# An xLSTM-like attention with a dense layer and eight experts on one core: another pairing of token blocks, another order of the first expert series, and 32-row parts on another engine

## The chip, the cores and the metric

The kernel runs on one core of one Trainium2 chip. A core has five engines that run beside each other, each with an instruction queue that it works through in order: TensorE (PE; its weight loads are shown apart as PEld), VectorE (DVE), ScalarE (ACT), GpSimd (POOL) and SyncE (SP), which here only issues transfers. The metric is device time in microseconds (us) of one execution, as the median of several runs.

## What is computed

Three parts follow one another, all in float32. Cut to what matters:

```python
# attention: 2 batches x 8 heads, 768 steps, head size 40, a scan over t
m_new = max(f_gate + m, i_gate); f, i = exp(f_gate + m - m_new), exp(i_gate - m_new)
C = f * C + i * outer(v, k);  n = f * n + i * k
y = sigmoid(o_gate) * (C @ q) / max(abs(n . q), 1)
# dense layer: x is 1536 tokens x 320
h = x @ w_in;  x = max(0.01 * h, h) @ w_out              # 320 -> 2048 -> 320
# experts: 8 of them, 320 -> 1024 -> 320
P = exp(x @ w_gate - max)                                # 1536 x 8
for _ in range(8):
    P /= P.sum(1) + 1e-9;  P /= P.sum(0) + 1e-9;  P *= 1536 / 8
out = sum(P[:, e] * (relu(x @ w1[e]) @ w2[e]) for e in range(8))
```

## The kernel before

Products of float32 matrices are made from a rounded part and what rounding left over: a value is split by ScalarE into a "high" copy and by VectorE or GpSimd into a "low" difference, and several matmuls add up high and low terms in one PSUM bank.

**Stage 1** (to about 280 us) holds attention and the dense layer. Attention is cut into 12 chunks of 128 tokens, 6 to a batch. The dense layer goes over six tiles j of 256 tokens; each tile takes 16 steps f over the 2048 inner columns, so there are 96 steps g = 16 j + f. A step has eight matmuls up (`ha`, line 201), a leaky relu on ScalarE (`leak`, `gg`, line 668), the split (`hha` on ScalarE, line 674, `hla`, line 679, on GpSimd from g = 32 on), and three steps later six products down for each of the tile's two blocks (`ya`, lines 208 to 210). From g = 32 on, work that doesn't belong to the dense layer hangs at a step, before or after its down: attention of the chunks 6 to 11 by the table `ATTEND` (a chunk's steps for decay, scores, values, rest and turn, counted from the first step of the tile before the one that it fills), and the preparation of the experts by calls of `step(g, function, ...)`. A chunk's values step has the products `yps` with the weighed scores (line 563; VectorE weighs them at line 553, writing to the large buffer `R`), `zps` (569) and `dps` (575), the state.

```python
            before[g_values] += [c.values, c.recall, c.state]
            after[g_values].append(c.attend_all)
```

**Stage 2** holds the experts. Each of the 8 experts is 4 units of 256 inner columns (`NU` = 32 units); the 1536 tokens are two halves q of three positions p, a position being a pair of 128-token blocks, so there are 64 series (n, q), in a fixed list that begins (0,0), (1,0), (2,0), (0,1), (1,1), (2,1). An in-series, `up_c(i)`, makes the hidden values of a unit by seven products of four matmuls (`b`, lines 963 to 966) in place of eight, with sums and differences of the blocks of both operands. Between the products ScalarE copies `s0` (line 988), VectorE adds `s1` (991), `s2` (994) and `c11`, `c10`, `c01` (982), ScalarE makes two relu copies of each (983, 984) and GpSimd the low part (985). An out-series, `down_c(i)`, makes six blocks `y` of 320 columns by six matmuls each, and VectorE adds them to `acc` (lines 1030 to 1036; the very first ones are plain copies, on ScalarE at line 1032 for the second half). In-series i + 1 runs ahead of out-series i.

Both operands need preparing. A position (class `Position`) copies part of its tokens (`repeat`, lines 733 and 1049), turns them by eight transposes (`px`, line 286, copied at 287), makes sums (line 293), and splits: high (258), low (261), and a 32-row part of its own, `rest7`, line 265, since half of the 320 columns is 128 + 32. A unit (class `Products`) does the same with its first weight, `load1`, `sums` (line 237) and `split1`, and with the second `load2` (line 230) and `split2`, high on ScalarE (249) and low (250). In stage 2 such work is hung at slots of a series by `when(g, slot, ...)`: slots 0 to 6 follow the products of in-series g + 1, slots 7 to 12 the blocks of out-series g. There the order of the code is the order of each queue. The weights P are made in stage 2 too: logits, row sums and column sums over 8 rounds hang at slots, and P is used from the second expert on.

Of the kernel before, what the change touches and what calls it, by code (L numbers as in the profile page):

```python
# [8 lines left out]
F32 = mybir.dt.float32  # L9
# [5 lines left out]
ALU = mybir.AluOpType  # L15
# [7 lines left out]

ATTEND = ((0, 2, 6, 11, 14), (5, 6, 10, 11, 14), (0, 3, 6, 8, 14), (5, 7, 8, 12, 14))
RUNS = ((0, 0, 6), (1, 0, 10), (0, 6, 14), (1, 10, 16), (0, 14, 16))
# [29 lines left out]
def mlstm_moe_kernel(ctx, tc, qp, q3, kp, kn, vn, gates_in, og, cst_in, scr_in, w_in, w_out, w_gate, w1, w2, out):  # L55
# [156 lines left out]
    class Products:  # L212
# [14 lines left out]

        def load2(self):
            self.raw2 = wp.tile([P, 2, DM], F32, tag="raw", name=f"raw2_{self.nm}", bufs=3)
            nc.sync.dma_start(self.raw2, self.src[1])  # L230
# [36 lines left out]
    class Position:  # L267
# [5 lines left out]
        def repeat(self, copy):  # L273
            self.rr = rrp.tile([P, 2, 2, P], F32, tag="rr", name=f"rr_{self.nm}", bufs=RRB[0])
            for i in range(2):
                x = x2s[self.q][:, i * HP + self.p, 2 * P:DM]
# [58 lines left out]
    with ExitStack() as st1:  # L335
# [399 lines left out]
        def step(g, fn, *args):  # L735
            after[g].append(lambda: fn(*args))
# [15 lines left out]
        for p in range(3):  # L752
            for k in range(2):
# [3 lines left out]
                step(g + 1, x0[p].rest, k, V)  # L757
        step(g5 + 5, experts[0].split1, 0, V, GP)
        step(g5 + 6, experts[0].split1, 1, V, GP)
# [3 lines left out]
        for k in range(4):  # L763
            step(g5 + 5 + k, experts[1].sums, V, (k,))
            step(g5 + 9 + k, experts[2].sums, V, (k,))
        step(g5 + 9, experts[1].split1, 0, V, GP)
        step(g5 + 10, experts[1].split1, 1, V, GP)
        step(g5 + 11, experts[0].split2, GP)
        step(g5 + 11, x1[0].repeat, copy_rest)
        step(g5 + 12, x1[0].turn, 0, ps_b)  # L770
        step(g5 + 13, x1[0].turn, 1, ps_b)
        step(g5 + 13, experts[2].split1, 0, V, GP)
        step(g5 + 14, experts[2].split1, 1, V, GP)
        step(g5 + 14, x1[0].sums, V, 0)
        step(g5 + 15, x1[0].sums, V, 1)
        step(g5 + 15, experts[1].load2)
        step(g5 + 16, experts[2].load2)

# [234 lines left out]
    def down_c(i):  # L1013
# [6 lines left out]
        for b in range(2):  # L1020
            for p in range(HP):
                t = b * HP + p
                k = ny[0] % 3
# [18 lines left out]
                at(i, 7 + t)  # L1042

# [19 lines left out]
    for p, sums, highs, lows, rests in ((0, None, ((-1, 0), (-1, 1)), ((-1, 3), (-1, 4)), ((-1, 3), (-1, 4))),  # L1063
                                        (1, ((-1, 6), (0, 3)), ((0, 7), (0, 8)), ((0, 10), (0, 11)), ((0, 9), (0, 11))),
                                        (2, ((0, 12), (1, 3)), ((1, 5), (1, 6)), ((1, 8), (1, 10)), ((1, 7), (1, 9)))):
        for k in range(2):
            if p:
                when(*sums[k], x1[p].sums, V, k)
            when(*highs[k], x1[p].high, k)
            when(*lows[k], x1[p].low, k, V)  # L1070
            when(*rests[k], x1[p].rest, k, GP)

    for g, s, q, i in ((1, 4, 0, 0), (1, 7, 0, 1), (2, 1, 1, 0), (2, 5, 1, 1)):
        when(g, s, logits, q, i)
    for g, s, fn in ((2, 8, logits_turn), (2, 9, logits_sum), (2, 11, top_turn), (2, 12, top_one), (3, 1, top_all), (3, 2, exps),
                     (3, 5, rows)):
        when(g, s, fn)
# [143 lines left out]
```

## Time and profile before

| what | value |
|---|---|
| runs | 955.83, 952.17, 953.15 us; median 953.15 |
| profiled execution | 953.82 us |
| its span, first to last instruction | 952.1 us |
| mean granted TensorE clock | 0.989 |
| TensorE busy | 936.0 us, 98% of the span |
| VectorE, ScalarE, GpSimd busy | 588.6, 495.7, 564.9 us |
| chain of work that ended last | TensorE 86%, VectorE 6%, transfers 3%, ScalarE 2% |

The span is what the profile shows; the 1.7 us of difference lie around it. A busy TensorE may still be slow: the granted clock is a share of 2.4 GHz, and it is told per slice. Starts in the rows are counted from the start of the span. Each row of a timeline has start, duration, engine, line, operation, what it writes and reads, and in brackets how long the engine stood still before it and which instruction ended that. Matmuls overlap, so the next one's start, not the duration, tells what one costs.

### The profile page before, as it was taken

To read this page: it belongs to the slowest core of one execution; us is meant where nothing else is said; L and a number is where in the kernel's file an instruction comes from. 1 tells how busy PE (TensorE), PEld (TensorE's weight loads), DVE (VectorE), ACT (ScalarE), POOL (GpSimd) and SP (SyncE) were. 2 spreads that over 40 slices of the span, in tenths; PEclk is the share of its full clock that TensorE was granted. 3 is DMA by queue.
4 is the path that set the end of the run, shared out by engine and by line. 5 is a ranking of instruction groups with operands and counts; after the bars stand their busy time and mean duration, and the time that the engine had idled before them with its cause. 6 is when DMAs were issued, how large, how long until landed. Compare 5 with 4: busy or idle time off the path is not lost.

```text
span 952.1 us, 16842 instructions
## 1 busy us (share of the span) xinstructions
PE 936.0 (98%) x6182; PEld 907.7 (95%) x6182; DVE 588.6 (62%) x1156; ACT 495.7 (52%) x968; POOL 564.9 (59%) x578
## 2 busy tenths in 40 slices
PE   8999999999999999999999999999999999999998
PEld 5799999999998999999999999999999999999998
DVE  6999742422747578556656556556556556656655
ACT  6886453353766454745445545445545445545442
POOL 0021253543566565776777777777777777777762
PEclk8799999999999999999999999999999999999999
DMA  9853130201200111111111111111111111111102
GB/s 298 265 183 106 39 100 19 68 17 39 59 29 23 37 37 37 37 37 54 42 50 37 38 37 54 42 51 37 38 37 54 42 50 37 38 37 55 32 1 83
DMA packets 57304, 56.50 MB, mean 59 GB/s; under 512 B 7574, under 2 KB 48006, under 8 KB 57222
## 3 DMA queue, kind: packets, MB, share of 16 engines
q1 hardware_dynamic: 57222, 55.43, 19.1%
q8 instruction: 48, 0.79, 0.3%
q14 instruction: 34, 0.28, 0.1%
HBM read 53.44 MB, written 1.97 MB: 58 GB/s over the span
## 4 chain that ended last, share of the span: by engine, by line
PE 86%; DVE 6%; DMA 3%; ACT 2%; issue 1%; SPq 1%; POOL 1%; DVEq 0%; ACTq 0%; POOLq 0%
PE y L208 12%; PE y L210 12%; PE y L209 12%; PE b L963 8%; PE b L966 8%; PE b L964 8%; PE b L965 8%; PE ha L201 7%; PE ya L208 2%; PE ya L210 2%; PE ya L209 2%; PE yps L563 1%; DMA raw_a<-in_w_out_dram 1%; DMA R<-in_kn_dram 1%; PE zps L569 1%
## 5 line engine op out<-in xcount | busy, mean ns | idle before, releaser
L985 POOL TENSOR_TENSOR hl<-c,hh 128x384 fp32r<-128x384 f32 x192 | 197.3, 1028 | 168.7 <-ACT c L984 145.9
L208 PE MATMUL y<-w_e,hh 128*128 128x320 f32 x768 | 238.2, 310 | 0.6 <-ACT acc L1032 0.6
L209 PE MATMUL y<-w_e,hh 128*128 128x320 f32 x768 | 236.9, 308 | 0.0
L210 PE MATMUL y<-w_e,hl 128*128 128x320 f32 x768 | 236.8, 308 | 0.0
L1036 DVE SCALAR_TENSOR_TENSOR acc<-y,Pg,acc 128x320 f32<-128x320 f32 x336 | 179.1, 548 | 63.1 <-PE y L210 56.3
L983 ACT ACTIVATE hh<-c 128x384 fp32r<-128x384 f32 x192 | 99.8, 520 | 207.4 <-DVE c L982 207.3
L963 PE MATMUL b<-X,w_e 128*128 128x384 f32 x448 | 152.9, 341 | 2.0 <-DVE s L994 1.5
L966 PE MATMUL b<-X,w_e 96*128 96x384 f32 x448 | 151.2, 338 | 0.0
L964 PE MATMUL b<-X,w_e 128*128 128x384 f32 x448 | 151.0, 337 | 0.0
L965 PE MATMUL b<-X,w_e 128*128 128x384 f32 x448 | 150.8, 337 | 0.0
L208 PEld LDWEIGHTS y<-w_e,hh 128*128 128x128 f32 x768 | 144.3, 188 | 2.0 <-ACT acc L1032 1.0
L209 PEld LDWEIGHTS y<-w_e,hh 128*128 128x128 f32 x768 | 144.2, 188 | 0.0
L210 PEld LDWEIGHTS y<-w_e,hl 128*128 128x128 f32 x768 | 144.1, 188 | 0.0
L984 ACT ACTIVATE c<-c 128x384 f32<-128x384 f32 x192 | 101.0, 526 | 18.4 <-ACT hh L983 1.5
L201 PE MATMUL ha<-xT,w_a 128*128 128x256 f32 x768 | 108.5, 285 | 1.1 <-DVE hla L679 0.8
L982 DVE TENSOR_TENSOR c<-b,s 128x384 f32<-128x384 f32 x192 | 100.7, 551 | 13.5 <-PE b L966 12.4
L201 PEld LDWEIGHTS ha<-xT,w_a 128*128 128x128 f32 x768 | 99.3, 190 | 4.6 <-DVE hla L679 2.0
L1001 DVE SCALAR_TENSOR_TENSOR hl<-b,hh 128x384 fp32r<-128x384 f32 x64 | 35.7, 558 | 95.2 <-ACT hh L1000 95.2
L963 PEld LDWEIGHTS b<-X,w_e 128*128 128x128 f32 x448 | 84.8, 189 | 3.3 <-DVE s L994 2.2
L237 POOL TENSOR_TENSOR raw_e<-raw_e 128x256 f32<-128x256 f32 x116 | 84.5, 738 | 4.6
L964 PEld LDWEIGHTS b<-X,w_e 128*128 128x128 f32 x448 | 85.2, 190 | 0.0
L966 PEld LDWEIGHTS b<-X,w_e 96*128 96x128 f32 x448 | 84.2, 188 | 0.6 <-POOL X L265 0.6
(189 smaller groups left out, 1487.2 us busy)
## 6 DMA issues: line engine op xcount, KB each, us to landing
raw_e<-in_w_dram SPq DMA_DIRECT2D x32, 320.0 KB, 2.9
raw_e<-in_w_dram SPq DMA_DIRECT2D x62, 128.0 KB, 2.2
raw_e<-in_w_dram SPq DMA_DIRECT2D x248, 32.0 KB, 1.9
raw_a<-in_w_in_dram SPq DMA_DIRECT2D x8, 768.0 KB, 6.1
R<-in_kp_dram SPq DMA_DIRECT2D x10, 256.0 KB, 3.2
R<-in_qp_dram SPq DMA_DIRECT2D x10, 256.0 KB, 3.6
raw_a<-in_w_out_dram SPq DMA_DIRECT2D x4, 640.0 KB, 3.8
rawU<-in_w_out_dram SPq DMA_DIRECT2D x4, 640.0 KB, 5.6
```

What stands on the lines that cost most here:

```text
L201: nc.tensor.matmul(h_ps, t1[:, ws, c * P:(c + 1) * P], xt[:, xs, t0:t0 + n], start=(j == 0), stop=(j == len(MM1) - 1),)
L208: nc.tensor.matmul(y_ps, a, t2[:, c, :], start=first, stop=False)
L209: nc.tensor.matmul(y_ps, a, t2[:, 2 + c, :], start=False, stop=False)
L210: nc.tensor.matmul(y_ps, b, t2[:, c, :], start=False, stop=last)
L963: nc.tensor.matmul(bank, f[:, 0], b[:, 0], start=fresh, stop=False, skip_group_check=not fresh)
L964: nc.tensor.matmul(bank, f[:, 0], b[:, 2], start=False, stop=False, skip_group_check=not fresh)
L965: nc.tensor.matmul(bank, f[:, 2], b[:, 0], start=False, stop=False, skip_group_check=not fresh)
L966: nc.tensor.matmul(bank, f[0:K3, 1], b[0:K3, 1], start=False, stop=True, skip_group_check=not fresh)
L982: nc.vector.tensor_tensor(c, part, plus, op=ALU.add)
L984: nc.scalar.activation(c, c, AF.Relu)
L985: nc.gpsimd.tensor_tensor(hl[a][b], c, hh[a][b].bitcast(F32), op=ALU.subtract)
L1036: nc.vector.scalar_tensor_tensor(out=o, in0=y, scalar=Pg[:, 2 * HP * q + t, e:e + 1], in1=o, op0=ALU.mult, op1=ALU.add)
```

## The change

1. Chunk b of tiles 3 to 5 (chunks 7, 9 and 11) has its values at step 9 instead of 8.
2. A position of the experts takes blocks 2p and 2p + 1 of its half, where it took blocks p and p + 3. So the second half's position 0 needs only tile 3, position 1 tile 4 and position 2 tile 5. Position 1's copies, transposes and sums move from stage 2 into stage 1, after position 0's, and position 2 gets the buffer `rawE`. The transposes of the logits and the order of the six blocks of an out-series follow.
3. The 32-row parts of units 0 to 2 and of the second half go to VectorE instead of GpSimd, and so do the second weights' lows of units 0 to 2. The second loads of units 1 and 2 are issued in stage 1 at steps 87 and 90 (they were at 95 and 96); unit 1's goes into the buffer `rawU`, which unit 0's first weight leaves, and unit 2's into that which unit 1's first weight leaves.
4. Out-series 2 runs ahead of in-series 3: in 0, in 1, out 0, in 2, out 1, out 2, in 3, in 4, out 3, and so on as before.
5. In series 0 and 3 the relu copies and the low part of c01 wait until the next series' s0 has been copied.
6. Of the first copies to `acc` of the second half, two of six go to VectorE.
7. The slots of the second half's splits, of the logits and of the rounds of P are new; the columns come half a series later.

```diff
-ATTEND = ((0, 2, 6, 11, 14), (5, 6, 10, 11, 14), (0, 3, 6, 8, 14), (5, 7, 8, 12, 14))
+ATTEND = ((0, 2, 6, 11, 14), (5, 6, 10, 11, 14), (0, 3, 6, 8, 14), (5, 7, 9, 12, 14))
...
-            xa, xb = (x2s[self.q][:, i * HP + self.p, :] for i in range(2))
+            xa, xb = (x2s[self.q][:, 2 * self.p + i, :] for i in range(2))
...
-        step(g5 + 5, experts[0].split1, 0, V, GP)
...
+        step(g5 + 5, experts[0].split1, 0, V, V)
...
+        step(g5 + 7, experts[1].load2, rawU[:, 0:2 * DM].rearrange("p (n w) -> p n w", n=2))
...
+        step(g5 + 9, experts[1].split1, 1, V, V)
+        step(g5 + 9, experts[0].split2, V)
...
+        step(g5 + 10, experts[1].split2, V)
+        step(g5 + 10, experts[2].load2)
...
+        step(g5 + 13, x1[1].repeat, copy_rest)
...
+        step(g5 + 14, experts[2].split2, V)
...
-    rrp, RRB[0] = cp, 2
+    rrp = cp
...
+    TWICE = (0, 3)
...
+            def split():
+                nc.scalar.activation(hh[a][b], c, AF.Relu)
+                nc.scalar.activation(c, c, AF.Relu)
+                nc.gpsimd.tensor_tensor(hl[a][b], c, hh[a][b].bitcast(F32), op=ALU.subtract)
+
+            if (a, b) == (0, 1) and i in TWICE:
+                held.append(split)
+            else:
+                split()
...
         nc.scalar.activation(p1, bank[0], AF.Copy)
+        while held:
+            held.pop()()
...
-                t = b * HP + p
+                t = 2 * p + b
...
-                if n == 0 and q == 0:
+                if n == 0 and b * HP + p in (0, 1, 2, 3, 4, 5) and q == 0 or n == 0 and b * HP + p in (0, 1) and q == 1:
...
-    for p in (1, 2):
-        when(-1, (0, 2)[p - 1], x1[p].repeat, copy_rest)
-    for g, s, p, k in ((-1, 2, 1, 0), (-1, 4, 1, 1), (0, 1, 2, 0), (0, 5, 2, 1)):
-        when(g, s, x1[p].turn, k, ps_s, rawE if p == 1 else None)
...
+    when(0, 7, x1[2].turn, 0, ps_s, rawE)
...
+        if i == 2:
+            down_c(i)
         if i + 1 < len(order):
             up_c(i + 1)
-        down_c(i)
+        if i != 2:
+            down_c(i)
```

TensorE's queue at chunk 7, in tile 2 (`ha40` is the up of step 40, `hha37` the high part of step 37; lines are those of before in rows without a sign or with -):

```order
 L210 MATMUL ya2_0_1_1472<-w2_a2_505,hla36_1499 128x320
 L201 MATMUL ha40_1642<-xT2_1314,w1_a4_643 128x256 x8
-L563 MATMUL yps_7_1657<-R0_75 128x41 x8
-L569 MATMUL zps_7_1666<-Cst1_102,R0_75 128x123 x3
-L575 MATMUL dps_7_1670<-R0_75 120x123 x3
 L208 MATMUL ya2_0_0_1471<-w2_a2_505,hha37_1526 128x320
 L209 MATMUL ya2_0_0_1471<-w2_a2_505,hha37_1526 128x320
```

and one step further on:

```order
 L210 MATMUL ya2_0_1_1472<-w2_a2_505,hla37_1527 128x320
-L201 MATMUL ha41_1706<-xT2_1314,w1_a4_643 128x256 x8
+L201 MATMUL ha41_1674<-xT2_1314,w1_a4_643 128x256 x8
+L563 MATMUL yps_7_1689<-R0_75 128x41 x8
+L569 MATMUL zps_7_1698<-Cst1_102,R0_75 128x123 x3
+L575 MATMUL dps_7_1702<-R0_75 120x123 x3
 L208 MATMUL ya2_0_0_1471<-w2_a3_694,hha38_1560 128x320
 L209 MATMUL ya2_0_0_1471<-w2_a3_694,hha38_1560 128x320
```

The values, recall and state of chunk 7 stood between the up of step 40 and the down of step 37; they now stand behind the up of step 41.

ScalarE's queue around step 89, near the end of stage 1, before (`w10_e0_2` is part of unit 2's first weight, `gg90` the leaky relu of step 90):

```order
L668 ACTIVATE gg89_3090<-ha89_3081 128x256
L258 ACTIVATE w10_e0_2_3217<-raw1_e0_2_2970 128x4x256
L674 ACTIVATE hha89_3092<-gg89_3090 128x256
L668 ACTIVATE gg90_3117<-ha90_3108 128x256
L674 ACTIVATE hha90_3119<-gg90_3117 128x256
L668 ACTIVATE gg91_3142<-ha91_3133 128x256
```

and with the change:

```order
L668 ACTIVATE gg89_3097<-ha89_3088 128x256
L258 ACTIVATE w10_e0_2_3204<-raw1_e0_2_2970 128x4x256
L674 ACTIVATE hha89_3099<-gg89_3097 128x256
L249 ACTIVATE w2_e0_2_3266<-raw2_e0_2_3144 128x640
L668 ACTIVATE gg90_3128<-ha90_3119 128x256
L674 ACTIVATE hha90_3130<-gg90_3128 128x256
L287 ACTIVATE rawx_1_0_3146<-px0_1_0_3147 128x4x128
L668 ACTIVATE gg91_3162<-ha91_3153 128x256
```

The rounding of unit 2's second weight, `w2_e0_2`, now stands ahead of `gg90`, and the copy of a position's transposes, `rawx`, ahead of `gg91`.

ScalarE's queue where in-series 1 begins, before (`hh10` and `hh01` are relu copies of series 0, `s0_1` the copy of series 1):

```order
L983 ACTIVATE hh10_0_3337<-c10_0_3404 128x384
L984 ACTIVATE c10_0_3404<-c10_0_3404 128x384
L983 ACTIVATE hh01_0_3336<-c01_0_3413 128x384
L984 ACTIVATE c01_0_3413<-c01_0_3413 128x384
L988 ACTIVATE s0_1_3432<-b0_1_3420 128x384
```

and with the change:

```order
L999 ACTIVATE hh10_0_3362<-c10_0_3411 128x384
L1000 ACTIVATE c10_0_3411<-c10_0_3411 128x384
L1009 ACTIVATE s0_1_3435<-b0_1_3423 128x384
L999 ACTIVATE hh01_0_3361<-c01_0_3421 128x384
L1000 ACTIVATE c01_0_3421<-c01_0_3421 128x384
```

`s0_1` has moved ahead of the two copies of c01 of series 0.

## Rows read from the trace of the kernel before

**Rows 1.** The page, part 1: busy time, share of the span, instructions of each engine.
```profile
PE 936.0 (98%) x6182; PEld 907.7 (95%) x6182; DVE 588.6 (62%) x1156; ACT 495.7 (52%) x968; POOL 564.9 (59%) x578
```

**Rows 2.** TensorE's waits: its line, releaser; us in total, times, longest.
```profile
PE yps L563 <- DVE R L553: 1.6, 3, 1.2
PE b L963 <- DVE s L994: 1.5, 2, 1.2
PE ya L210 <- POOL hla L679: 0.9, 2, 0.7
PE y L208 <- ACT acc L1032: 0.6, 1, 0.6
```

**Rows 3.** Busy time in a window: us, PE PEld DVE ACT POOL, PEclk, DMA.
```profile
600.00:625.00 25.00, 25.00 (x159) 25.00 (x158) 15.53 (x30) 12.90 (x25) 17.13 (x19) 1.00 0.12 36
```

**Rows 4.** TensorE's timeline around chunk 7: start, duration, instruction, count [idle before, releaser].
```profile
136.82 0.80 PE L575 MATMUL dps<-R 128*120 128x123 f32 x6
137.38 0.40 PE L209 MATMUL ya<-w_a,hha 128*128 128x320 f32 x1
140.87 1.10 PE L201 MATMUL ha<-xT,w_a 128*128 128x256 f32 x8
143.19 0.41 PE L563 MATMUL yps<-R 128*128 128x41 f32 x2 [1.23 <-DVE R L553]
143.79 1.76 PE L563 MATMUL yps<-R 128*128 128x41 f32 x14 [0.18 <-DVE R L553]
146.12 1.42 PE L575 MATMUL dps<-R 128*120 128x123 f32 x6
150.17 0.31 PE L208 MATMUL ya<-w_a,hha 128*128 128x320 f32 x1
151.05 1.10 PE L201 MATMUL ha<-xT,w_a 128*128 128x256 f32 x8
151.99 0.31 PE L208 MATMUL ya<-w_a,hha 128*128 128x320 f32 x1
```

**Rows 5.** VectorE's timeline, the weighing of chunk 7.
```profile
142.46 1.28 DVE L553 TENSOR_TENSOR R<-sps,R 128x512 f32<-128x512 f32 x2
```

**Rows 6.** Busy time and granted clock in the window behind it.
```profile
145.00:150.00 5.00, 5.00 (x30) 5.00 (x30) 2.81 (x10) 0.00 (x0) 0.72 (x1) 0.66 0.28 78
```

**Rows 7.** TensorE's timeline at the end of stage 1.
```profile
261.16 0.31 PE L209 MATMUL ya<-w_a,hha 128*128 128x320 f32 x1
262.12 0.41 PE L210 MATMUL ya<-w_a,hla 128*128 128x320 f32 x1 [0.66 <-POOL hla L679]
...
270.39 0.42 PE L210 MATMUL ya<-w_a,hla 128*128 128x320 f32 x1 [0.28 <-POOL hla L679]
```

**Rows 8.** GpSimd's timeline, same stretch.
```profile
259.46 1.74 POOL L265 TENSOR_TENSOR w_e<-raw_e,w_e 32x512 fp32r<-32x512 f32 x1 [2.52 <-issue]
```

**Rows 9.** VectorE's timeline, same stretch.
```profile
244.73 0.68 DVE L265 TENSOR_TENSOR X<-rawx,X 32x512 fp32r<-32x512 f32 x1
...
251.23 1.67 DVE L265 TENSOR_TENSOR X<-rawx,X 32x512 fp32r<-32x512 f32 x1
...
257.02 0.41 DVE L237 TENSOR_TENSOR raw_e<-raw_e 128x256 f32<-128x256 f32 x1
```

**Rows 10.** DMA issues from 240 to 300 us: count, KB each, median us to landing.
```profile
raw_e<-in_w_dram SPq DMA_DIRECT2D x3, 320.0 KB, 3.1
```

**Rows 11.** ScalarE's timeline at the end of stage 1.
```profile
261.56 0.72 ACT L249 ACTIVATE w_e<-raw_e 128x640 fp32r<-128x640 f32 x1
262.19 0.37 ACT L668 ACTIVATE gg<-ha 128x256 f32<-128x256 f32 x1
```

**Rows 12.** TensorE's timeline in the second and third in-series.
```profile
289.84 0.45 PE L963 MATMUL b<-X,w_e 128*128 128x384 f32 x1 [0.55 <-ACT s L988]
...
304.26 0.44 PE L963 MATMUL b<-X,w_e 128*128 128x384 f32 x1 [1.19 <-DVE s L994]
```

**Rows 13.** VectorE's timeline in the third in-series.
```profile
300.54 2.53 DVE L293 TENSOR_TENSOR rawx<-rawx 128x256 f32<-128x256 f32 x2
```

More of the change, by code (lines that the diff above doesn't have):

```diff
@@ L226, in load1, with load2 @@
                     nc.sync.dma_start(dst[r * KM:(r + 1) * KM, h, :, 1], src[h * KM:(h + 1) * KM, 2])
-        def load2(self):
-            self.raw2 = wp.tile([P, 2, DM], F32, tag="raw", name=f"raw2_{self.nm}", bufs=3)
+        def load2(self, home=None):
+            self.raw2 = wp.tile([P, 2, DM], F32, tag="raw", name=f"raw2_{self.nm}", bufs=3) if home is None else home
             nc.sync.dma_start(self.raw2, self.src[1])
@@ L275, in repeat @@
             for i in range(2):
-                x = x2s[self.q][:, i * HP + self.p, 2 * P:DM]
+                x = x2s[self.q][:, 2 * self.p + i, 2 * P:DM]
                 copy(self.rr[:, i].rearrange("p h (r k) -> p h r k", r=4),
@@ L757, in mlstm_moe_kernel @@
                 step(g + 1, x0[p].rest, k, V)
-        step(g5 + 5, experts[0].split1, 0, V, GP)
-        step(g5 + 6, experts[0].split1, 1, V, GP)
         step(g5 + 2, experts[1].load1)
@@ L762, in mlstm_moe_kernel @@
         step(g5 + 6, experts[0].load2)
[L763 to L777, printed above, removed]
+        step(g5 + 5, experts[0].split1, 0, V, V)
+        step(g5 + 5, experts[1].sums, V, (0,))
+        step(g5 + 6, experts[0].split1, 1, V, V)
+        step(g5 + 6, experts[1].sums, V, (1,))
+        step(g5 + 7, experts[1].load2, rawU[:, 0:2 * DM].rearrange("p (n w) -> p n w", n=2))
+        step(g5 + 7, experts[1].sums, V, (2,))
+        step(g5 + 8, experts[1].sums, V, (3,))
+        step(g5 + 8, experts[2].sums, V, (0,))
+        step(g5 + 8, experts[1].split1, 0, V, V)
+        step(g5 + 9, experts[2].sums, V, (1,))
+        step(g5 + 9, experts[1].split1, 1, V, V)
+        step(g5 + 9, experts[0].split2, V)
+        step(g5 + 9, x1[0].repeat, copy_rest)
+        step(g5 + 10, experts[2].sums, V, (2,))
+        step(g5 + 10, experts[1].split2, V)
+        step(g5 + 10, experts[2].load2)
+        step(g5 + 10, x1[0].turn, 0, ps_b)
+        step(g5 + 11, experts[2].sums, V, (3,))
+        step(g5 + 11, x1[0].turn, 1, ps_b)
+        step(g5 + 12, x1[0].sums, V, 0)
+        step(g5 + 12, experts[2].split1, 0, V, V)
+        step(g5 + 13, x1[0].sums, V, 1)
+        step(g5 + 13, x1[1].repeat, copy_rest)
+        step(g5 + 13, experts[2].split1, 1, V, V)
+        step(g5 + 14, x1[1].turn, 0, ps_b)
+        step(g5 + 14, experts[2].split2, V)
+        step(g5 + 15, x1[1].turn, 1, ps_b)
+        step(g5 + 16, x1[1].sums, V, 0)
+        step(g5 + 17, x1[1].sums, V, 1)
         zero = places["dm"].rearrange("p g f -> p (g f)").bitcast(BF16)
@@ L897, in logits_turn @@
         for t in range(NCK):
-            nc.tensor.transpose(ltp[:, t].rearrange("p a e -> p (a e)"), lT[:, t * P:(t + 1) * P], ident[0:2 * E, 0:2 * E])
+            c = (2 * (t // (2 * HP)) + t % 2) * NQ + t % (2 * HP) // 2 * P
+            nc.tensor.transpose(ltp[:, t].rearrange("p a e -> p (a e)"), lT[:, c:c + P], ident[0:2 * E, 0:2 * E])
     def logits_sum():
@@ L966, in product @@
         nc.tensor.matmul(bank, f[0:K3, 1], b[0:K3, 1], start=False, stop=True, skip_group_check=not fresh)
-    hidden = {}
+    hidden, held = {}, []
     def up_c(i):
@@ L1041, in down_c @@
                     nc.sync.dma_start(out[row:row + P, :], o)
-                at(i, 7 + t)
+                at(i, 7 + b * HP + p)
     def scale_first(q, t):
@@ L1056, in mlstm_moe_kernel @@
     rawE = cp.tile([P, 7, 2 * P], F32, tag="rawE", name="rawE")
-    for p in (1, 2):
-        when(-1, (0, 2)[p - 1], x1[p].repeat, copy_rest)
-    for g, s, p, k in ((-1, 2, 1, 0), (-1, 4, 1, 1), (0, 1, 2, 0), (0, 5, 2, 1)):
-        when(g, s, x1[p].turn, k, ps_s, rawE if p == 1 else None)
[L1063 to L1077, printed above, removed]
+    when(-1, 0, x1[2].repeat, copy_rest)
+    when(-1, 0, x1[0].high, 0)
+    when(-1, 1, x1[0].high, 1)
+    when(-1, 3, x1[0].low, 0, V)
+    when(-1, 5, x1[0].low, 1, V)
+    when(0, 7, x1[2].turn, 0, ps_s, rawE)
@@ new lines, in mlstm_moe_kernel @@
+    when(0, 9, x1[0].rest, 0, V)
+    when(0, 9, x1[1].high, 0)
+    when(0, 10, x1[1].high, 1)
+    when(0, 11, x1[2].turn, 1, ps_s)
+    when(0, 11, x1[0].rest, 1, V)
+    when(0, 11, x1[1].low, 0, V)
+    when(0, 12, x1[1].low, 1, V)
+    when(0, 12, x1[1].rest, 0, V)
+    when(1, 4, x1[2].sums, V, 0)
+    when(1, 4, logits, 0, 0)
+    when(1, 7, x1[2].sums, V, 1)
+    when(1, 8, logits, 0, 1)
+    when(1, 9, x1[1].rest, 1, V)
+    when(1, 9, x1[2].high, 0)
+    when(1, 10, x1[2].high, 1)
+    when(1, 11, x1[2].low, 0, V)
@@ L1079, in mlstm_moe_kernel @@
+    when(1, 12, x1[2].low, 1, V)
+    when(2, 1, logits, 1, 0)
+    when(2, 5, logits, 1, 1)
+    when(2, 7, x1[2].rest, 0, V)
+    when(2, 8, x1[2].rest, 1, V)
+    when(3, 1, logits_turn)
+    when(3, 2, logits_sum)
+    when(3, 4, top_turn)
+    when(3, 5, top_one)
+    when(3, 8, top_all)
+    when(3, 9, exps)
+    when(3, 11, rows)
     for it in range(8):
-        g = 3 + (it + 1) // 2
-        for s, fn in zip(((8, 9, 11), (2, 3, 3))[it % 2], (lambda it=it: columns(it), columns_end, rows)):
+        g = 4 + it // 2
+        for s, fn in zip(((2, 3, 3), (8, 9, 11))[it % 2], (lambda it=it: columns(it), columns_end, rows)):
@@ L1086, in mlstm_moe_kernel @@
             when(8 + q, (0, 0, 1, 1, 2, 2)[t], scale_first, q, t)
-    when(0, 4, experts[1].split2, GP)
-    when(0, 12, experts[2].split2, GP)
     for n in range(3, NU):
```

3 lines of the change are left out of this document (removed).

## The prediction, made before the changed kernel had run

> **What bounds the kernel now.** I read the page's busy times first. TensorE works 936.0 of 952.1 us [rows 1], so the change can only win what TensorE loses to stops and to a slower clock; it runs the same matrix products in both kernels, so no work goes. The profiled execution took 953.82 us, 1.72 more than its span and 0.67 above the median of the runs, 953.15. I make the sum against 953.82 and take 0.67 off at the end.
>
> Next the table of TensorE's waits, to see where stops are [rows 2]: on VectorE's R of line 553 (1.6 us), on s of line 994 (1.5), on GpSimd's hla of line 679 (0.9) and on ScalarE's acc of line 1032 (0.6). Then a stretch well inside the experts: TensorE is busy for 25.00 of 25 us at full clock, while VectorE works 15.53 [rows 3]. Nothing is to be won there. All that the change can reach lies before about 340 us, and I went through TensorE's timeline there.
>
> A stop costs more than the wait that is printed. In [rows 7] the matmul at 262.12 follows one that began at 261.16. The wait printed is 0.66, but a matmul of this shape is due 0.15 later (six of them take 0.88 in [rows 4], 150.17 to 151.05), so 0.81 is lost, and the matmul itself takes 0.41 instead of 0.31. I therefore put each stop at its printed wait and 0.25 more.
>
> **Chunk 7's values one step later.** At 140.87 the eight ha matmuls begin, and eight of them take 0.94 (151.05 to 151.99), so the values could begin at 141.81. They begin at 143.19, and after two of them stop again until 143.79 [rows 4]. Both wait for the weighing on VectorE, two instructions from 142.46 that end at 143.74 [rows 5]. Two values matmuls would have been done some 0.2 after 141.81, so the loss is 143.79 - 141.81 - 0.2 = 1.8. What the change puts in front is a down step and the next ha, 0.88 and 0.94, so the values would be asked for at 141.81 + 1.82 = 143.63, against 143.74 for the last piece. The stop goes but for about 0.1: **+1.7**. Chunks 9 and 11 move too, without a stop to lose. The price of the later values is that recall, state and what VectorE makes of them come a step later; the normalising has its own steps after that, and chunk 7's turn stays five steps behind, so I cost it at nothing (if that cover were gone, at most the 1.82 moved would come back).
>
> Behind this stop the clock falls. From 145 to 150 us the granted clock averages 0.66 of full [rows 6]; full is 2.4 GHz, and the stretch lies mostly at the lower level of 1.2. From 146.12 to 150.17 TensorE does dps, one down step and one ha, 4.05 us. The same at full clock is 0.56 (136.82 to 137.38), 0.88 and 0.94, with some 0.1 of the stretch being dps matmuls that stand on either side: 2.5. Without the stop ahead of it I expect the clock to stay up: **+1.55**. The low end is nothing, if the clock falls for another reason.
>
> **The 32-row parts leave GpSimd.** A 32-row part takes GpSimd 1.74 at 259.46 [rows 8], and hla, which TensorE needs, stands behind it. That is the stop of 0.66 at 262.12 and of 0.28 at 270.39: with 0.25 each, 1.44. After the change GpSimd holds nothing but hla there, so both go. On VectorE the part costs what a full one does, 0.68 at 244.73, and 1.67 at 251.23 when GpSimd reads too [rows 9]. VectorE's list up to the last part of expert 1 becomes 27 instructions from 244.73 on. Eight of them are sums at 0.41 (257.02), the others at most 0.68 where nothing else reads: 16.2 in all, 0.60 each. Before, the 13 instructions from there to 257.02 took 0.945 each. I take 0.70, nearer the bare price because GpSimd has half as much to do there, though its hla stays: 18.9, to 263.6. Who waits for that list? Expert 2's second load goes into the buffer that it frees, 3.1 to landing [rows 10], so 266.7. ScalarE's rounding of it (line 249) now stands **in front of gg90** on ScalarE's queue, and ha92 on TensorE waits for gg90's bank. Line 249 and gg take 0.72 and 0.37 [rows 11]: 267.8. When is ha92 due, in times of before? The matmul that stops at 270.39 was due at 269.95, ha92 began 1.24 ahead of that (its 0.94 and two matmuls), and the stop at 262.12 had cost 0.9: 267.8 as well. So I charge 0.35 for this and for the sums of expert 1 coming a little later: **+1.1**. The best is 1.44 and some smaller stops around it that I have not summed (0.6 in all).
>
> **Series 0 to 2.** In the second in-series TensorE stops at 289.84 for ScalarE's s, whose instruction stood behind two relu copies, printed 0.55; the next product but one stops for s of line 994, which has 1.5 in two stops, and 1.19 of it stands in the third in-series, so about 0.3 here [rows 2, 12]. With 0.25 each: 1.35. The change lets s0 pass ahead of hh01 and c01. The products after that still wait for VectorE's s1 and s2 in turn, so I keep rather more than one of the stops: **+0.5** (ends 0 and 1.35). In the third, the stop of 1.19 at 304.26 comes from VectorE's two sums of 2.53 that stand ahead of s1 at 300.54 [rows 12, 13]. Those of position 1 are done in stage 1 now, and those of position 2 sit at another slot behind. The stop goes with its 0.25: **+1.45** (ends 0 and 1.45).
>
> **Out 1 and out 2 in a row, and the columns half a series later.** The stop of 0.6 for acc [rows 2] goes, as does its 0.25, since ScalarE no longer holds the first two copies. Against it two out-series run with no in-series between, in which VectorE takes six accumulations each and also the four 32-row parts and lows of X1; and mean, exponent and first rows of the weights bring short waits of their own at new places. VectorE has over a third of its time free in [rows 3], so I put the new stops at 0.75 against the 0.85: **+0.1** (ends -1.5 and +0.85). The other edits (the first lows of X1, expert 0's low on VectorE) lie in VectorE time after 264, where it waited for others; nothing.
>
> **Sum.** 1.7 + 1.55 + 1.1 + 0.5 + 1.45 + 0.1 = 6.4. 953.82 - 6.4 = 947.4; less 0.67 is **946.7 us**.
>
> **Rivals.**
> *ScalarE stuck in front of gg90 (slower).* If VectorE's 27 instructions take 0.945 each, as the 13 did, the list ends at 270.2, the load lands at 273.3, and ha92 can start at 274.4 instead of 267.8. The 6.6 lost, of which 0.35 is charged already, use up the gain: 953.0. From a mean of 0.95 on (6.8 us over 27 on top of 0.70) it is slower than before, by 0.5% from 1.13. For it speaks that 0.945 was measured here; against it, that those 13 had GpSimd's own first 32-row parts beside them, which now are gone. Chance 0.08, half of it or a little more beyond 957.9 if another wait is added.
> The Trainium skill (SBUF — State Buffer, section Who interferes with whom) speaks against the move in just this place: a VectorE instruction with two inputs in SBUF contends with a GpSimd instruction that reads SBUF, and one blocks the other. By that rule alone, every one of the list that meets an hla waits for it to end. The 1.67 against 0.68 in [rows 9] agrees.
>
> *The clock still falls.* The stretch of half speed stays, or comes at another stop: 1.55 is not won, 948.3. For it speaks that the cause of the fall is only placed by its time behind the stop; against it, that the clock stands at full in the long stretch of [rows 3], where there is no stop. Chance 0.15.
> The Trainium skill (TensorE: Matmul & The Clock Gate, Part 1) says that the throttled clock is the default and that activity releases it, by a monitor that doesn't run in step with the kernel. The clock of 0.66 right behind the longest stop agrees; that it may differ from run to run, no row here shows.
>
> *Stage 2 gives it back.* VectorE or ScalarE is late at new places and the 0.5, 1.45 and 0.1 come out at nothing: 948.8; with a new stop of 1.5 where out 2 ends, 950.3. For it: the same instructions still have to be done in about the same stretch, and VectorE gets 15 more in all. Chance 0.17.
>
> *The change doesn't do it:* the order of VectorE, ScalarE and TensorE does move as written; what could be is that the values stop again a step later for the same weighing. Then 1.7 and 1.55 stay lost: 950.0. Chance 0.03.
>
> **The numbers.** The forecast has 0.57. Its own range is 945.5 to 948.2. About 0.5% of the median, 4.8 us, is what a measurement of this kernel can tell from no change, so faster means below 948.4. Faster: the forecast and most of the clock's case, 0.71; same: stage 2, the failed shift and the milder half of the first rival, 0.25; slower 0.04. The range reaches down to 944.4 (both in-series stops, 0.84, the smaller stops near hla, 0.6, and 0.75 in the out-series) and up to 950.3 (stage 2 gives it back, with a new stop).
>
> **What would show it.** Right: no wait of yps on line 553 for chunk 7, and a clock of 1.00 from 145 to 150 us; no wait on hla after 255 us; no stop of 1.2 in the product behind the logits of series 2. Wrong: a stop of ha before step 92 with ScalarE's gg as releaser and line 249 in front of it (the first rival); a slice of clock below 1.00 behind 130 us (the second); waits of b or y on VectorE between 295 and 345 us that add up to over 2 us (the third).

## The result and the profile after

The changed kernel takes **946.57 us** (median of six runs, 945.12 to 949.48), the kernel before in the same series 954.49 (six runs, 952.17 to 960.08). The ratio is 0.9912, 95% interval 0.9888 to 0.9935; when it was measured once more, 0.9929 (0.9910 to 0.9949). Forecast were 946.7, a range of 944.4 to 950.3, and faster by over 0.5% with 0.71. The profiled execution took 945.96 us, its span 944.2.

Page, part 1, of the changed kernel:

```profile
PE 932.1 (99%) x6182; PEld 906.4 (96%) x6182; DVE 593.8 (63%) x1175; ACT 494.6 (52%) x966; POOL 544.2 (58%) x561
```

TensorE is busy 3.9 us less than in [rows 1], though it does the same 6182 instructions; part of it is the stretch at half clock, which counted as busy. GpSimd has 17 instructions fewer and VectorE 19 more (the prediction's third rival counted 15).

The wait table of TensorE, the rows that answer to [rows 2]:

```profile
PE ha L201 <- ACT gg L668: 0.8, 1, 0.8
...
PE yps L563 <- DVE R L553: 0.2, 1, 0.2
PE b L977 <- DVE s L1017: 0.2, 1, 0.2
```

The stops on hla at line 679 by GpSimd and on acc are gone, those on s have fallen from 1.5 to 0.2, and a new one of 0.8 has come, on ScalarE's gg. The 0.2 of yps is at another chunk.

TensorE at chunk 7 (columns as in [rows 4]), then the windows that answer to [rows 6]:

```profile
141.30 1.10 PE L201 MATMUL ha<-xT,w_a 128*128 128x256 f32 x8
143.12 1.12 PE L201 MATMUL ha<-xT,w_a 128*128 128x256 f32 x8
144.07 1.87 PE L563 MATMUL yps<-R 128*128 128x41 f32 x16
146.52 0.80 PE L575 MATMUL dps<-R 128*120 128x123 f32 x6
147.08 0.40 PE L208 MATMUL ya<-w_a,hha 128*128 128x320 f32 x1
148.06 1.11 PE L201 MATMUL ha<-xT,w_a 128*128 128x256 f32 x8
149.00 0.31 PE L208 MATMUL ya<-w_a,hha 128*128 128x320 f32 x1
```

```profile
140.00:145.00 5.00, 5.00 (x46) 4.88 (x42) 4.44 (x11) 1.68 (x5) 2.21 (x3) 1.00 0.48 144
145.00:150.00 5.00, 5.00 (x42) 5.00 (x42) 2.62 (x10) 0.87 (x3) 1.45 (x2) 1.00 0.25 75
```

The values begin at 144.07, right behind the ha at 143.12, without a stop; dps takes 0.56 (146.52 to 147.08) where it took 1.07 (146.12 to 147.19), and the clock stays at 1.00.

The end of stage 1: VectorE's list, the second load of unit 2 on SyncE's queue, ScalarE's rounding of it, and the ha of step 92 on TensorE:

```profile
241.74 0.68 DVE L265 TENSOR_TENSOR X<-rawx,X 32x512 fp32r<-32x512 f32 x1
...
257.84 2.53 DVE L237 TENSOR_TENSOR raw_e<-raw_e 128x256 f32<-128x256 f32 x4
...
261.41 0.55 DVE L265 TENSOR_TENSOR w_e<-raw_e,w_e 32x384 fp32r<-32x384 f32 x1
```

```profile
262.02 0.33 SPq L230 DMA_DIRECT2D raw_e<-in_w_dram  x1
```

```profile
264.88 0.74 ACT L249 ACTIVATE w_e<-raw_e 128x640 fp32r<-128x640 f32 x1 [3.25 <-DMA raw_e<-in_w_dram]
```

```profile
262.29 0.60 PE L286 MATMUL px<-cst,x 128*128 128x128 f32 x4
262.64 1.18 PE L201 MATMUL ha<-xT,w_a 128*128 128x256 f32 x8
...
264.54 0.60 PE L286 MATMUL px<-cst,rr 128*128 128x128 f32 x4
265.94 1.21 PE L201 MATMUL ha<-xT,w_a 128*128 128x256 f32 x8 [0.80 <-ACT gg L668]
```

VectorE's 27 instructions run from 241.74 to 261.96, 0.75 each. The load is issued at 262.02, and ScalarE stands still for 3.25 us until it has landed. ha92 starts 1.40 behind the transposes ahead of it, where the ha at 262.64 starts 0.35 behind its own: it is 1.05 late. (The expectations of the runs below have 0.97 for this stop; counted from start to start it is 1.05.)

What is left in in-series 1, in place of the 289.84 of [rows 12]:

```profile
282.74 0.44 PE L977 MATMUL b<-X,w_e 128*128 128x384 f32 x1
...
285.95 0.44 PE L977 MATMUL b<-X,w_e 128*128 128x384 f32 x1 [0.16 <-DVE s L1017]
```

Milestones of TensorE's timeline, in us from the start of each span. Between them the two kernels differ by the part of the change that lies there; what the first 140 us differ by is no part of it.

| start of | before | changed | difference | gained since the row above |
|---|---|---|---|---|
| ha ahead of chunk 7's old place | 140.87 | 141.30 | +0.43 | |
| ha two steps on | 151.05 | 148.06 | -2.99 | 3.42 |
| in 0 | 280.12 | 276.90 | -3.22 | 0.23 |
| out 0 | 293.07 | 287.47 | -5.60 | 2.38 |
| in 2 | 298.34 | 293.63 | -4.71 | -0.89 |
| in 5 | 339.74 | 331.65 | -8.09 | 3.38 |
| last matmul | 948.49 | 940.58 | -7.91 | -0.18 |

Two of the differences are only moved work. A group of four transposes costs about 0.44 (0.36 to the next start and the slower start behind it); four groups left in 0 and in 1, two of them for stage 1 and two for out 0. So stage 1's tail gained about 0.23 + 0.88 = 1.1, in 0 and in 1 about 2.38 - 1.76 = 0.6, and out 0 nothing.

### The profile page after: what moved, and what is told of

It reads as the page before. It is cut to its first block, busy times and chain, and to the rows that moved or that the text cites. A ratio compares the mean times of both kernels' runs of the same rounds, so it can differ in the third digit from the quotient of the medians.

```text
span 944.2 us, 16842 instructions
## 1 busy us (share of the span) xinstructions
PE 932.1 (99%) x6182; PEld 906.4 (96%) x6182; DVE 593.8 (63%) x1175; ACT 494.6 (52%) x966; POOL 544.2 (58%) x561
## 4 chain that ended last, share of the span: by engine, by line
PE 87%; DVE 4%; DMA 3%; ACT 3%; issue 1%; SPq 1%; POOL 0%; DVEq 0%; ACTq 0%
PE y L208 12%; PE y L209 12%; PE y L210 12%; PE b L977 8%; PE b L978 8%; PE b L980 8%; PE b L979 8%; PE ha L201 7%; PE ya L208 2%; PE ya L210 2%; PE ya L209 2%; PE yps L563 1%; DMA raw_e<-in_w_dram 1%; DMA sc<-in_gates_dram 1%; PE zps L569 1%
## 5 line engine op out<-in xcount | busy, mean ns | idle before, releaser
L679 POOL TENSOR_TENSOR hla<-gg,hha 128x256 fp32r<-128x256 f32 x64 | 48.7, 761 | 71.1 <-ACT hha L674 64.1
```

## The experiments

Below, a stretch of a run is compared with the same stretch of the changed kernel by TensorE's timeline: from chunk 7's first values product to in 0 (132.83 there, 132.96 when it was profiled again), and from in 0 to out 0 (10.57, 10.54). These repeat within 0.15 us, while the changed kernel's median moved by 1 us from one series to the next. The four runs of a series shared their runs of before: medians 954.67, 954.41 and 952.97.

### One digit on the kernel before, and back in the changed one

```diff
-ATTEND = (..., (5, 7, 8, 12, 14))
+ATTEND = (..., (5, 7, 9, 12, 14))
```

> The kernel before with one digit changed: chunk 7, 9 and 11's values a step later. My theory (the stop of 1.74 us at chunk 7 goes, and the stretch at half clock behind it goes with it): about 3.3 us faster than before; no wait of yps on line 553 at chunk 7, granted clock 1.00 from 145 to 150 us. Rival (the clock falls for another reason than that stop): about 1.7 us faster, and a slice of clock well below 1.00 stays between 143 and 152 us.

951.06 us, ratio 0.9974 (0.9956 to 0.9992), 3.6 less than the median of before. No wait on yps at chunk 7 is left, and the clock is 1.00 from 140 to 155 us:

```profile
141.27 1.12 PE L201 MATMUL ha<-xT,w_a 128*128 128x256 f32 x8
142.23 1.87 PE L563 MATMUL yps<-R 128*128 128x41 f32 x16
```

```profile
145.00:150.00 5.00, 5.00 (x41) 5.00 (x40) 2.87 (x10) 1.53 (x4) 1.51 (x2) 1.00 0.27 75
```

From the ha ahead of the old place to in 0 it takes 135.83 in place of 139.25, 3.42 less. My theory holds.

```diff
-ATTEND = (..., (5, 7, 9, 12, 14))
+ATTEND = (..., (5, 7, 8, 12, 14))
```

> The changed kernel with that one digit put back. My theory: about 3.3 us slower than the changed kernel (about 949.9 in all), the stop and the stretch at half clock are back, 1.7 and 1.6 us. Rival (in the changed kernel the weighing is early anyway, or the clock stays up): at most 1.7 us slower.

949.05 us, ratio 0.9944 (0.9922 to 0.9966), 2.5 above the changed kernel's 946.57 of another series. By the trace, from the ha ahead of the old place (139.55) to in 0 (278.63), it takes 139.08 in place of 135.60, 3.5 more. Stop and clock are back, in the first values row and the windows of this run:

```profile
141.94 0.42 PE L563 MATMUL yps<-R 128*128 128x41 f32 x2 [1.29 <-DVE R L553]
```

```profile
140.00:145.00 5.00, 3.53 (x29) 3.21 (x28) 2.81 (x6) 0.80 (x2) 1.32 (x2) 0.98 0.28 93
145.00:150.00 5.00, 5.00 (x29) 5.00 (x29) 3.08 (x10) 0.78 (x2) 0.72 (x1) 0.68 0.30 76
```

The yps stop is 1.29 and 0.18 as printed, 1.8 in all. So the stop and the fall of the clock come and go together, in either kernel.

### The new stop: unit 2's second weight elsewhere

```diff
-        step(g5 + 14, experts[2].split2, V)
...
+    when(0, 12, experts[2].split2, GP)
```

> The changed kernel with the second weight of unit 2 rounded in out-series 0, its low part on GpSimd there, in place of in front of gg90. My theory (ScalarE, held there by the transfer, makes TensorE stop 0.97 us before ha92): that stop goes and nothing takes its place, about 1.0 us faster than the changed kernel, 945.5. Rival (the next thing in ScalarE's queue, the copy of the transposes in front of gg91, which needs the buffer that VectorE's low of unit 0 leaves, holds it as long): no change, a stop before ha92 or ha93 stays.

945.17 us (944.14 to 946.56), ratio 0.9900 (0.9879 to 0.9921). From the values to in 0 it takes 131.72, 1.1 less than the changed kernel, and no wait on gg stands in the table. The rival's wait is there, on ScalarE's queue, but short:

```profile
262.44 0.60 ACT L287 ACTIVATE rawx<-px 128x512 f32<-128x512 f32 x1 [0.85 <-DVE w_e L250]
```

It is the copy of the transposes, held 0.85 by VectorE's low of unit 0, and it delays no matmul. Something does take the stop's place later, though: in 2 takes 0.38 more (291.64 to 297.98, against 293.63 to 299.59), part of which comes back behind it. From the values to the last matmul 0.9 is left of the 1.1 (795.57 against 796.51). The medians (945.17 against 946.57 and 945.56) can't tell the two kernels apart. Out-series 0 is also where the kernel before had this rounding, in the same slot and with its low on GpSimd, so this run takes back one part of the change, and that part cost time.

```diff
-        step(g5 + 14, experts[2].split2, V)
...
+    when(-1, 4, experts[2].split2, V)
```

> As the run before, but rounded on ScalarE and its low part on VectorE in in-series 0. My theory: the stop before ha92 goes as well (1.0 us), and the two instructions of some 0.7 and 0.8 us between the products of in-series 0 cost at most 0.3: 945.5 to 945.8. Rival (they push s0 of series 1 or s2 back by their length, as the sums did in the kernel before): 0.5 to 0.8 us lost in in-series 1, so nearly no change against the changed kernel.

946.45 us, ratio 0.9923 (0.9894 to 0.9951). The stop before ha92 is gone, but in 0 and in 1 take 11.38, 0.81 more. ScalarE's rounding and TensorE's stop in this run:

```profile
285.21 0.73 ACT L249 ACTIVATE w_e<-raw_e 128x640 fp32r<-128x640 f32 x1
```

```profile
287.31 0.44 PE L976 MATMUL b<-X,w_e 128*128 128x384 f32 x1 [0.32 <-DVE c L995]
```

VectorE's low (0.83) stands ahead of c10 there, c10 comes late, and with it a bank. The rival is right in its size, though it is c10 and not s0 or s2 that is pushed back: the loss of 0.81 is about what the low lasts. The rounding delays nothing by itself, since ScalarE stands still for 1.36 us behind it until c10 is there.

### The 32-row parts of units 0 to 2 back on GpSimd

```diff
-        step(g5 + 5, experts[0].split1, 0, V, V)
+        step(g5 + 5, experts[0].split1, 0, V, GP)
...
```

(the same in the other five calls)

> The changed kernel with the six 32-row parts of units 0 to 2 back on GpSimd, X's stay on VectorE. My theory: the stops on hla come back, at least two between 255 and 268 us, 1.4 to 2.1 us together; the stop before ha92 stays within 0.5 of its 0.97, since the buffer that the load waits for is now freed by GpSimd's part, behind two hla; 1 to 2 us slower than the changed kernel. Rival (what the kernel before lost there came from VectorE and GpSimd reading at once, and VectorE's list, four instructions shorter, gives as much back as the stops cost): within 0.5 us of the changed kernel, the stop before ha92 gone.

947.35 us, ratio 0.9935 (0.9911 to 0.9960); values to in 0 take 132.95, as in the changed kernel. My theory falls. One stop on hla is back (0.65 printed, 0.92 in all), and the one before ha92 is gone but for 0.16 instead, because TensorE now gets there later. VectorE's list, four instructions shorter, is no sooner done: the load is issued at 261.66, 118.2 after the values began, against 262.02 and 117.95. GpSimd's part, VectorE's four sums beside it, and the load:

```profile
255.66 1.75 POOL L265 TENSOR_TENSOR w_e<-raw_e,w_e 32x512 fp32r<-32x512 f32 x1 [2.31 <-issue]
```

```profile
256.17 4.41 DVE L237 TENSOR_TENSOR raw_e<-raw_e 128x256 f32<-128x256 f32 x4
```

```profile
261.66 0.33 SPq L230 DMA_DIRECT2D raw_e<-in_w_dram  x1
```

The four sums take 4.41; in the changed kernel, where GpSimd has only hla, 2.53. Four instructions of 0.55 to 0.68 (their time where nothing else reads) would have saved 2.5; the sums alone took 1.88 more while GpSimd's parts read beside them.

### No copies held back

```diff
-    TWICE = (0, 3)
+    TWICE = ()
```

> The changed kernel with no relu copies of c01 held back in series 0 and 3. My theory: s0 of series 1 stands behind two copies again, TensorE stops for it in the second product of in-series 1 by 0.4 to 0.8 us, and the later stop of 0.3 stays: 0.4 to 0.9 us slower than the changed kernel. Rival (the stop in the kernel before came from the copies of the transposes that ScalarE also did there, which are elsewhere now): within 0.2 us, and no new stop on s0.

946.01 us (945.20 to 950.56), ratio 0.9933 (0.9911 to 0.9954). The median can't show it; the trace does. In 0 and in 1 take 11.52, 0.95 more, and the stop on s0 is in the wait table, about as long as it was before (0.57 printed, 0.55 in [rows 12]):

```profile
PE b L977 <- ACT s L1009: 0.6, 1, 0.6
```

My theory holds, a little above its upper end, since the later stop grew as well, from 0.41 to 0.54.

### The old order of the series

```diff
-        if i == 2:
-            down_c(i)
         if i + 1 < len(order):
             up_c(i + 1)
-        if i != 2:
-            down_c(i)
+        down_c(i)
...
-    when(2, 7, x1[2].rest, 0, V)
-    when(2, 8, x1[2].rest, 1, V)
+    when(1, 12, x1[2].rest, 0, V)
+    when(1, 12, x1[2].rest, 1, V)
```

> The changed kernel with the series in the old order, in 3 ahead of out 2; the last two 32-row parts of X1 move from out-series 2 to the end of out-series 1, since in 3 needs them. My theory (out 2 ahead of in 3 gives VectorE the time to finish X1): TensorE stops where in 3 begins, for four VectorE instructions of 0.55 to 0.7 us behind the last y: 2.0 to 2.8 us slower than the changed kernel. Rival (the gain behind in 2 comes from ScalarE's copies to acc and the new slots, and the order matters little): within 0.5 us.

947.85 us, ratio 0.9944 (0.9924 to 0.9964), 1.3 to 2.3 above the changed kernel. From in 2 to in 5 it takes 39.85 (293.37 to 333.22), against 38.02 there and 41.40 in the kernel before. The loss is in two stops where in 3 begins, on X1's low and on its 32-row part:

```profile
306.97 0.44 PE L978 MATMUL b<-X,w_e 128*128 128x384 f32 x1 [0.47 <-DVE X L261]
...
308.67 0.44 PE L980 MATMUL b<-X,w_e 96*128 96x384 f32 x1 [1.08 <-DVE X L265]
```

With what they add, 1.86. My theory holds, just below its range.

### A longer list on VectorE

```diff
             rest7(*x, KM, rest)
+            if self.nm == "e0_1":
+                rest7(*x, KM, rest)
+                rest7(*x, KM, rest)
```

> The changed kernel with the two 32-row parts of unit 1 done three times over, four instructions more on VectorE that write the same values (four of 0.55 to 0.7 us, and two of unit 0's and 1's second lows that now stand among them). It doubles the suspected cost, VectorE's list ahead of unit 2's second load. My theory: the stop before ha92 grows by the full length, 2.4 to 4.5 us, to 3.4 to 5.5, and the clock falls behind it as it did behind chunk 7, another 1 to 2 us: 3 to 6 us slower than the changed kernel. Rival (the stop was the transfer's own, or VectorE had slack there): at most 1 us slower. If the stop grows and the clock stays at 1.00 behind it, the fall at chunk 7 was not the stop's alone.

946.86 us, ratio 0.9935 (0.9909 to 0.9961). What releases the load, the load, the stop and the windows behind it:

```profile
261.35 0.83 DVE L253 TENSOR_TENSOR w_e<-raw_e,w_e 128x640 fp32r<-128x640 f32 x1
```

```profile
262.20 0.33 SPq L230 DMA_DIRECT2D raw_e<-in_w_dram  x1
```

```profile
266.88 1.22 PE L201 MATMUL ha<-xT,w_a 128*128 128x256 f32 x8 [1.41 <-ACT gg L671]
```

```profile
265.00:270.00 5.00, 3.59 (x28) 3.33 (x27) 4.92 (x9) 4.71 (x11) 2.31 (x3) 1.00 0.00 0
270.00:275.00 5.00, 5.00 (x40) 4.99 (x39) 3.33 (x6) 2.80 (x6) 2.67 (x4) 1.00 0.21 59
```

The load is issued 119.7 after the values began, 1.76 later than in the changed kernel, but the stop grew only from 1.05 to 1.57. My size was wrong twice. Two 32-row parts of unit 1 stand behind the load: its wait ends no longer with the last of them, as in the changed kernel, but with VectorE's low of unit 0's second weight. And the order of ScalarE's queue moved: the rounding stands behind gg90 now, so that the next ha is held, which is due 2.0 later; against that an hha and a copy of transposes now stand between the rounding and the gg that frees the bank, 0.8 more. The clock stays at 1.00.

```diff
+            for _ in range(6 if self.nm == "e0_1" else 0):
+                rest7(*x, KM, rest)
```

> The long list once more, twelve more 32-row parts of unit 1 on VectorE, 7 to 9 us. Here ScalarE's rounding stands behind hha91. If the wait before ha runs through VectorE's list, the buffer and the load, one for one after about 2 us of slack: a stop of 3 to 6 us before ha93 or ha94, and 3 to 6 us slower than the changed kernel. On the clock: in the run with four more, a stop of 1.57 us left it at 1.00. If a long enough stop is what makes it fall, the clock falls behind this one, another 1 to 2 us; if it is the values products behind the stop, it stays at 1.00 here too.

952.90 us, ratio 1.0000 (0.9982 to 1.0018), 7.3 above the changed kernel in the same series.

```profile
273.55 0.33 SPq L230 DMA_DIRECT2D raw_e<-in_w_dram  x1
```

```profile
276.51 0.74 ACT L251 ACTIVATE w_e<-raw_e 128x640 fp32r<-128x640 f32 x1 [6.80 <-DMA raw_e<-in_w_dram]
...
278.61 0.39 ACT L670 ACTIVATE gg<-ha 128x256 f32<-128x256 f32 x1
```

```profile
279.06 2.08 PE L201 MATMUL ha<-xT,w_a 128*128 128x256 f32 x8 [5.29 <-ACT gg L670]
```

```profile
275.00:280.00 5.00, 0.94 (x4) 0.94 (x5) 4.80 (x11) 3.09 (x7) 0.00 (x0) 0.90 0.12 46
280.00:285.00 5.00, 5.00 (x33) 4.98 (x32) 4.26 (x6) 2.92 (x8) 3.26 (x3) 0.76 0.01 3
```

A matmul that came 5.00 later than in the changed kernel (the ha at 252.22, there 247.22) dates this run's rows: in the changed kernel's time the load, which again follows unit 0's second low, is issued at 268.55, 6.5 later, and the rounding of it begins 6.6 later. The stop is 5.45, 4.4 more than 1.05. Three terms make that up: 6.6 for the load; 1.5 because two copies of transposes now stand between the rounding and the gg that frees the bank (276.51 to 278.61, against 264.88 to 265.52 there); and 3.7 less because the ha that is held is now two steps on, ha94. So beyond the slack of these two steps a late load is paid one for one. From the values to in 0 the run takes 138.89, 6.0 more than the changed kernel. Here the clock falls, 0.90 and 0.76, and from 279.06 to 282.27 most of an ha and the matmuls down behind it run at about half pace.

### A shorter stop at chunk 7, which became a longer one

```diff
-ATTEND = (..., (5, 7, 9, 12, 14))
+ATTEND = (..., (5, 7, 8, 12, 14))
...
-            step(g + 2, x0[p].sums, V, 0)
-            step(g + 3, x0[p].sums, V, 1)
+            step(g + 2, x0[p].sums, V if p else GP, 0)
+            step(g + 3, x0[p].sums, V if p else GP, 1)
```

> The changed kernel with the values of chunk 7 back at step 8, and the four sums of X0's position 0 on GpSimd in place of VectorE, so that the weighing of chunk 7 comes 0.4 to 1.2 us sooner. It shortens the stop of 1.7 us without taking it away. If the stop's length makes the clock fall: with a stop of 0.6 to 1.3 the clock stays at 1.00 from 142 to 152 us, and only the shorter stop is lost. Rival (the light values products make it fall after any stop there): the clock falls again, a slice of 0.6 to 0.7, and 1.5 us with it.

951.26 us, ratio 0.9994 (0.9971 to 1.0017). It did not do what it was for. GpSimd's three sums stand ahead of its normalising of chunk 6 (line 596), for which VectorE's line 599 waits, ahead of the weighing:

```profile
139.10 2.46 POOL L293 TENSOR_TENSOR rawx<-rawx 128x256 f32<-128x256 f32 x3
...
141.51 0.72 POOL L596 TENSOR_TENSOR R<-R,den 128x320 f32<-128x320 f32 x1
```

```profile
142.27 0.99 DVE L599 TENSOR_TENSOR R<-R 128x320 f32<-128x320 f32 x1 [1.38 <-POOL R L596]
```

```profile
143.92 0.42 PE L563 MATMUL yps<-R 128*128 128x41 f32 x2 [2.56 <-DVE R L553]
```

```profile
145.00:150.00 5.00, 5.00 (x31) 5.00 (x31) 2.06 (x7) 0.00 (x0) 0.00 (x0) 0.66 0.17 43
```

The first stop is 2.7 in place of 1.4, the clock falls as it did with the shorter one. Whether a stop of about 1 us there would spare the clock stays open.

### The lows of X1 moved as well

```diff
-    when(-1, 3, x1[0].low, 0, V)
-    when(-1, 5, x1[0].low, 1, V)
+    when(0, 7, x1[0].low, 0, V)
+    when(0, 8, x1[0].low, 1, V)
...
-    when(0, 11, x1[1].low, 0, V)
-    when(0, 12, x1[1].low, 1, V)
-    when(0, 12, x1[1].rest, 0, V)
+    when(1, 5, x1[1].low, 0, V)
+    when(1, 6, x1[1].low, 1, V)
+    when(1, 6, x1[1].rest, 0, V)
```

(with unit 2's second weight in out-series 0, as above)

> The changed kernel with unit 2's second weight rounded in out-series 0 as above, and X1's lows of position 0 moved from in 0 and in 1 to out 0, those of position 1 from out 0 to in 2. My theory (the two stops of 0.3 and 0.4 us left in in-series 1 come from VectorE's lows standing ahead of hl00 and s2): in-series 0 and 1 take 9.9 to 10.2 us in place of 10.57, the stop before ha92 is gone: 1.2 to 1.8 us faster than the changed kernel. Rival (s2 waits for s1 whatever stands ahead, and the lows in in 2 make a stop there): in-series 0 and 1 at 10.4 to 10.6, no faster than the run with the rounding alone.

947.18 us, ratio 0.9945 (0.9923 to 0.9967). In 0 and in 1 take 10.56, as before the move; the rival is right that the lows don't make those stops. And out 1 gets new ones, 1.5 with what they add:

```profile
PE y L208 <- DVE acc L1056: 1.2, 2, 0.8
```

### The changed kernel again

> The changed kernel once more, as a measure for the three runs beside it: 946 to 947.5 us, the stop before ha92 0.8 to 1.2 us, clock 1.00 from 100 us on.

945.56 us (944.58 to 948.31); stop before ha92 1.13 (0.87 printed), the clock at 1.00 from 100 us on.

## Why the prediction was right

**The values a step later: right, in size too.** 1.7 + 1.55 = 3.25 were forecast, 3.42 came, and the one digit alone gives 3.42 on the kernel before. That the clock's fall goes with the stop is shown both ways round (one digit on, one digit off).

**The 32-row parts leave GpSimd, +1.1: right as a sum, wrong as a reason.** The tail gained 1.1. But two stops on hla were priced at 1.44 and put down to those parts alone. With the parts of units 0 to 2 back on GpSimd one stop on hla is back, and the same stretch is as short all the same. The new stop before ha92, which I charged with 0.35, took 1.05 to 1.13: the list took 0.75 an instruction, not 0.70, and ended 1.3 us later than that. What then made the tail shorter than before is not shown by a run of its own; unit 0's second low also left GpSimd there (1.88 us on GpSimd, 1.25 on VectorE), and no run put it back alone. The sign that I had named for the first rival, a stop before ha92 with line 249 in front of gg, did appear, at 1.05 in place of the 6.6 that would have made the change useless. The longest list shows that its price is real: one for one beyond the slack, 4.4 us of stop there.

The rule of the Trainium skill that I set against the move (SBUF — State Buffer, Who interferes with whom) bears on this term in a way I had not used: VectorE's two-input instruction and GpSimd's read exclude each other, so an instruction taken off GpSimd gives VectorE time back. The 4.41 against 2.53 for the same four sums agrees.

**In 1, +0.5: right** (0.6 in all; holding the copies is worth 0.95 by the run without it, so the rest of the change costs some 0.3 there). **In 2, +1.45: right in the trace**, the stop of 1.19 is not in the table any more; it was not undone alone.

**Out 1 and out 2 in a row, +0.1: this is the term that was mis-sized.** From in 2 to in 5 the kernel gained 3.38; without in 2's 1.45 that is 1.9. The step that failed is "I put the new stops at 0.75 against the 0.85". New stops came to about half of that at most (0.23 before the transpose of the logits' maximum, the rest late starts of 0.1), and the old ones were more than the 0.85 I had from the wait table: late starts on X1's last parts between 313 and 315 us (0.4) and ahead of the logits (0.2) carry no wait there, and the columns' 0.33 I had left out. The run with the old order puts 1.83 of it on the order itself: VectorE needs out 2's time for X1. Waits on VectorE of over 2 us between 295 and 345, the third rival's sign, did not come.

**The sum.** By terms 6.4 was forecast and 8.3 came from 140 us on; the first 140 us were 0.4 slower in the profiled execution of the changed kernel, and its median lies 0.6 above that execution, while the one of before moved from 953.15 to 954.49 with more runs. So 946.7 against 946.57 is closer than the terms are, and that closeness is luck. (The lower end of the range, 946.7 less 0.84, 0.6 and 0.75, comes to 944.5 and not 944.4.)

## What to carry to other kernels

Before an operation moves from GpSimd to VectorE, price what GpSimd's reads cost VectorE in the same stretch: here six parts moved and VectorE's list took no longer. Look for what stands behind a transfer on an in-order queue: an early rounding that waits for a load held a bank that TensorE needed, and rounding it in out-series 0 instead, where it was before, was worth 1.1 us there and 0.9 by the end. Effects of 1 us are settled by stretches of the trace between two matmuls, not by medians.

## What was not expected of the hardware

What length of stop makes the clock fall is not shown. Behind 1.05 us before ha92 and 1.57 before ha93 it stayed at 1.00, and so it did behind the 1.19 of [rows 12]; behind 1.4 and 0.4 ahead of chunk 7's values it fell, to 0.66 over the next 5 us window; behind 5.45 before ha94, with no values near, it fell too. So the values' small matmuls are not needed for a fall. The 1.57 is longer than the first stop at chunk 7 but shorter than the two there together, 1.8, and the run that should have shortened that stop made it longer; whether the length alone decides stays open. The Trainium skill (TensorE: Matmul & The Clock Gate, Part 1) has the array throttled by default and released by activity; that fits all of these rows and decides none.

The executions of one kernel spread by 2 to 10 us. Two of the traces are of long ones, 950.00 and 956.95 us, and in both the clock stood at half once more between 40 and 54 us. The window from 25 to 50 us of the changed kernel, and of the run with the rounding in in-series 0, which took 950.00 in its profiled execution:

```profile
25.00:50.00 25.00, 22.08 (x152) 18.17 (x151) 23.72 (x44) 20.62 (x34) 0.74 (x1) 0.84 0.80 244
```

```profile
25.00:50.00 25.00, 21.82 (x111) 18.29 (x112) 20.03 (x37) 17.30 (x27) 0.74 (x1) 0.64 0.80 242
```

Its clock there is 0.64, and it has 111 matmuls done in place of 152. Chunk 7's values begin at 148.47 and 148.95 in these two, against 144.07 in the changed kernel: what they lost lies in a stretch that the change does not touch; where the other long executions lost theirs is not shown.
